# Filler products from TensorE's first instruction on, s and b as single words, and a new order of priorities in a fused attention and feed-forward kernel

## The chip, the cores and the metric

The kernel runs on one core of a Trainium2 chip. The metric is the device time of one execution in microseconds (us). TensorE (PE) multiplies, VectorE (DVE) and ScalarE (ACT) evacuate and transform, GpSimd (POOL) issues the loads that cast to 16 bits and does some copies, and SyncE (SP) issues the other DMAs.

## The reference

Attention over 8 batches and 8 heads, with a local mask in heads 0 to 3 and a strided mask in heads 4 to 7. Its output is the input of a feed-forward layer with a squared ReLU, scaled by `s` and shifted by `b`.

```python
# q, k, v: (8, 8, 576, 64); w_in: (512, 2048); w_out: (2048, 512); s, b: (1,)
scores = matmul(q, k.T) / 8
mask_local   = (rel >= 0) & (rel < 32)                 # heads 0..3, rel = row - column
mask_strided = (rel >= 0) & (row % 32 == column % 32)  # heads 4..7
attn = softmax(where(mask, scores, -1e9)) @ v
x = attn.transpose(0, 2, 1, 3).reshape(4608, 512)
h = x @ w_in
g = s * maximum(h, 0) ** 2 + b
out = g @ w_out                                        # (4608, 512) float32
```

## The kernel before

**Work.** A batch has four pairs of heads, m = 0 to 3 (0 and 1 local, 2 and 3 strided). For each pair TensorE transposes q and k (later batches, from 3 to 5 on, get this from a transposing DMA instead), makes scores against a block-diagonal copy of q (`qD_loc`, `qD_str`), ScalarE takes the exponential (`p_loc`, `p_str`), VectorE masks it (batch 0 is masked by an extra product instead), TensorE multiplies with v, which has a column of ones, and VectorE divides by that column's sums (`rec`, then `x_nat`). A transpose puts the result into `xT`.

The feed-forward layer takes the 4608 tokens in blocks T of 512. Its first product (`ff1`) has, for each of 16 slices ft of the hidden width, four products over ct (the four pairs' channels), each of 512 columns; ScalarE's ReLU gives `u`, a square gives `gT`. In the first block, ft = 0 to 3 runs with ct outermost (`FIRST`), so that its products for ct = 0 need pair 0's `xT` only. The second product (`ff2`) has 64 products of 512 columns for a block; from block 2 on (`SEVEN`) seven products of blocks take the place of eight, and so does the first product in the last two blocks. `s` is used as a per-partition scalar when the output is evacuated, `b` scales the column sums of `w_out` into `bcs`.

**Order.** The order of instructions on every engine is fixed when the kernel is built, by a planner (`Plan`, L17). It keeps a clock `t` for TensorE in ns, a time at which each other engine is free, and a table `done` of when each piece of data is there. TensorE's work comes as `Step`s with a duration, needs and a PSUM bank; evacuations come as posts with a cost for each engine that may do them. `flush` gives a post to an engine when its needs are met and the engine is free within `SLACK` of the clock; among posts that are ready, the one with the smallest ready time plus its kind's `LATER` goes first. The kind is the first entry of its key, and a key whose third entry is 0 gets nothing added. Kinds: `e` exponentials, `p` masks (in batch 0 exponentials), `u` ReLUs, `g` squares, `ev` output evacuations, `in` casts and copies of inputs, and others for the products in seven.

The main loop takes a step of attention when one is ready and attention is behind its share (`due`), else a step of `ff1`, else of `ff2`. When nothing is ready it fills TensorE with products of constants, which nothing reads (`keep_running`, L1416 on), until the next thing is expected; this is done only while fewer than 16 steps of `ff1` are out. Loads have expected landing times: a table `AT` for batch 0 (the first q at 5200), and for what follows `landing(cost)`, which adds costs to a running `ring`. The first quarter of w_in costs 2700 and gets 600 on top. The planner starts at `plan.t = 1850.0` (L1414).

**Loads at the start.** GpSimd's queue issues q, k and v of batch 0, then casts v, then issues the four quarters of w_in (`load_w_in`, L339), later batch 1 and w_out. SP's queue issues, after a small copy that waits for part of q (`gate`, L1293), the masks, then s and b, then rows of zeros for `ks` (L311):

```python
nc.sync.dma_start(out=masks, in_=h_mask.ap())
nc.sync.dma_start(out=s_sb, in_=moe_s.to_broadcast([128, 1]))
nc.sync.dma_start(out=b_sb, in_=moe_b.to_broadcast([128, 1]))
```

So s and b are each read 128 times, a word for each partition.

Lines that the prediction uses: L439 and L447 transposes of q and k, L568 scores, L629 products with v, L676 transposes of x, L928 `ff1`, L1183 `ff2`, L896 and L1153 the products in seven, L1431 fillers, L586 exponentials, L646 and L656 the division, L349 copies and casts, L1210 and L1221 the column sums of w_out.

Of the kernel before, what the change touches and what calls it, by code (L numbers as in the profile page):

```python
# [1 line left out]

# [1 line left out]

# [7 lines left out]
FP32 = mybir.dt.float32  # L12
AF = mybir.ActivationFunctionType
# [3 lines left out]
class Plan:  # L17
# [6 lines left out]

    LAT = {"A": 70.0, "V": 70.0, "P": 70.0, "D": 12000.0, "X": 7000.0, "Y": 12000.0}

    SLACK = 800.0
    LATER = {"g": 1500.0, "S": 1500.0, "in": 2500.0, "w_mix": 2500.0, "wc": 1500.0}

    def __init__(self):  # L30
        self.t = 0.0
        self.done = {}
        self.pend = []
        self.free = {"A": 0.0, "V": 0.0, "P": 7000.0, "D": 0.0, "X": 0.0, "Y": 0.0}
        self.banks = {}
# [9 lines left out]
    def flush(self):  # L45
        while True:
            best = None
            for p in self.pend:
# [3 lines left out]
                if p[1].keys() <= {"A", "V"} and min(  # L52
                        self.free[e] for e in p[1]) > self.t + self.SLACK:
                    continue
# [66 lines left out]
        self.keys, self.posts, self.after = keys, posts, after  # L121


@with_exitstack
def kernel(
    ctx: ExitStack,
# [7 lines left out]
    moe_b: bass.AP,  # L134
    out: bass.AP,
):
    nc = tc.nc
    B, H, S, D = q.shape
    NTOK, DM = out.shape
    DFF = moe_w_in.shape[1]  # L140
    stride = 32
    scale = 1.0 / float(np.sqrt(D))
    PS = 512
# [14 lines left out]
    for p in range(SQ):  # L158
        for c in range(SQ):
# [12 lines left out]
    const = ctx.enter_context(tc.tile_pool(name="consts", bufs=1))  # L172
# [11 lines left out]
    ident = const.tile([128, 128], FP16)  # L184
    masks = const.tile([128, LQ + SQ], FP16)
    mask_loc, mask_str = masks[:, 0:LQ], masks[0:SQ, LQ:LQ + SQ]
    s_sb = const.tile([128, 1], FP32)
    b_sb = const.tile([128, 1], FP32)

    w_in_sb = [const.tile([128, 4, n], FP16, name=f"w_in_sb{i}")  # L190
               for i, n in enumerate((512, 512, 512, 512))]
    w_out_sb = const.tile([128, NFT, DM], FP16)
    bcs = const.tile([128, DM], FP32)
    w_mix = {i: const.tile([128, NFT // 2, DM // 2], FP16, name=f"w_mix{i}") for i in (2, 3, 4)}
# [3 lines left out]
    part32 = w_mix[4].rearrange("p f m -> p (f m)").bitcast(FP32)[:, 64:192]  # L198
# [30 lines left out]
    x_dram = [tc.dram_tile([S, 128], FP16, name=f"x_dram{i}") for i in range(4)]  # L229

    sched = ctx.enter_context(tc.manual_schedule())
    plan = Plan()

# [102 lines left out]
    def load_w_in():  # L336
        wv = moe_w_in.rearrange("(c p) f -> p c f", p=128)
        for i, at in enumerate((0, 512, 1024, 1536)):
            nc.gpsimd.dma_start(out=w_in_sb[i], in_=wv[:, :, at:at + w_in_sb[i].shape[2]])  # L339

    def load_w_out(chunks):

# [48 lines left out]
    TB, SB, AB, F1B, F2B = 1, 2, 1, 2, 2  # L391
# [24 lines left out]
    def bank(group):  # L416
        return ps[group.name]

    def pair_steps(b, m):
# [6 lines left out]
        st = {}  # L426
# [128 lines left out]
        def score(i, group):  # L555

            g, n = i // per_s, min(per_s, nt - i // per_s * per_s)

            def f():
                if i % per_s == 0:  # L560
                    st["s", g] = bank(group)
                c = i % per_s * 2 * nq
                if b < PE_MASK:

                    nc.tensor.matmul(
                        out=st["s", g][0:nk, c:c + 2 * nq], lhsT=ident[0:nk, 0:nk],
                        rhs=neg_loc if loc else neg_str, start=True, stop=False)
                nc.tensor.matmul(  # L568
                    out=st["s", g][0:nk, c:c + 2 * nq], lhsT=(st["k"][:, i * nq:i * nq + nk] if loc else st["k"][:, i, 0:SQ]),
                    rhs=st["q"][:, i].rearrange("d e c -> d (e c)"), start=b >= PE_MASK, stop=True)  # L570

            s = Step(f, (2 if b < PE_MASK else 1) * (2 * nq / 2.4 + 8), needs=[("q", id_), ("k", id_)],
                     group=group if i % per_s == 0 else None)
            if i % per_s == n - 1:
                key = ("s", id_, g)
                s.keys = [key]

                ng = nt // per_s + (nt % per_s > 0)

                def ex(eng):  # L580
                    if g == 0:
                        st["whole"] = p_bufs[loc][p_taken[loc] % len(p_bufs[loc])]
                        p_taken[loc] += 1
                    at = g * 2 * per_s * nq
                    st["pw", g] = st["whole"][:, at:]
                    nc.scalar.activation(  # L586
                        out=st["pw", g][0:nk, 0:2 * n * nq],
                        in_=st["s", g][0:nk, 0:2 * n * nq], func=AF.Exp, scale=scale)

                def ms(eng):  # L590
                    pt = st["whole"][:, 0:2 * nt * nq].rearrange("k (t c) -> k t c", c=nq)
                    mask = (mask_loc if loc else mask_str)[:, None, :].to_broadcast(
                        [nk, 2 * nt, nq])
                    nc.vector.tensor_tensor(out=pt[0:nk], in0=pt[0:nk], in1=mask, op=ALU.mult)
# [132 lines left out]
    gts = {}  # L727
# [5 lines left out]
    H = NFT // 2  # L733
# [496 lines left out]
        return first, second, third  # L1230


    def arrive(keys, at):
        for k in keys:
            plan.done[k] = at

    ring = 0.0
# [53 lines left out]
    def after_landing(i, src):  # L1291
# [5 lines left out]
        out=v_loc[0].rearrange("p h t d -> p (h t) d")[LPAD:128, 2 * LT:4 * LT, 0:D],  # L1297
        in_=v.rearrange("b h (t p) d -> b p (h t) d", p=LQ)[0, :, 2 * LT:4 * LT])
# [9 lines left out]
    plan.done["raw", "v", False, 0] = AT["vs"]  # L1308
    after_landing(0, loaded[0, "ql"][0:1, NL // 2:NL // 2 + 1])
    nc.sync.dma_start(out=masks, in_=h_mask.ap())  # L1310
    nc.sync.dma_start(out=s_sb, in_=moe_s.to_broadcast([128, 1]))
    nc.sync.dma_start(out=b_sb, in_=moe_b.to_broadcast([128, 1]))
    def weights_in(eng):

        nonlocal ring
        nc.gpsimd.tensor_copy(out=gate[0:8, 2:3], in_=loaded[0, "qs"][64:SQ, 0:1])
        load_w_in()
        ring = 14200.0
        for keys, cost in ([0], 2700), ([1], 2500), ([2], 2500), ([3], 2500):
            arrive([("w_in", c) for c in keys], landing(cost))  # L1320

# [51 lines left out]
    f1, f2 = [], []  # L1373
    for T in range(NBLK):
        if T == 0:

            gr = [Group("s", SB, "f1", F1B) for _ in range(4)]
            cts = FIRST
            f1 += [ff1(T, ft, ct, gr[ft], cts, True) for ct in cts for ft in range(4)]
        for ft in ff_order(T)[0 if T else 4:] if T < FIRST7 else ():  # L1380
            gr = Group("f1", F1B, "f2", F2B) if T == 0 else Group("f1", F1B)
            for ct in range(4):
                f1.append(ff1(T, ft, ct, gr))
        if T == FIRST7:
            f1 += ff1_seven()
        if T == 0:

            gr = [Group(*x) for x in [("f2", F2B), ("f2", F2B), ("s", SB), ("f2", F2B)]]
            sums = bcs_steps(Group("s", SB))
            for c in range(0, NFT, 4):  # L1390
                if c >= NFT - 8:
                    f2.append(sums[c // 4 - 2])
                f2 += [ff2(T, ts, ft, gr[ts]) for ts in range(2) for ft in range(c, c + 4)]
            f2.append(sums[2])
            f2 += [ff2(T, ts, ft, gr[ts]) for ts in (2, 3) for ft in range(NFT)]
            for i, s in enumerate(f2):
                s.pos = 1.25 * (i + 1) / len(f2)
            mix_post()
            continue
        if T >= SEVEN:  # L1400
            f2 += ff2_seven(T)
            continue
        for ts in range(4):

            parts = 2 if T == NBLK - 1 and ts == 3 else 1
            for part in range(parts):
                gr = Group("f2", F2B)
                for ft in range(NFT):
                    f2.append(ff2(T, ts, ft, gr, part, parts))
                    f2[-1].pos = T + 0.25 + (ts + (part + ft / NFT) / parts) / 4  # L1410
    combine_w()
    for T in range(FIRST7, NBLK):
        combine_x(T)
    plan.t = 1850.0  # L1414

    def keep_running(until):  # L1416

# [20 lines left out]
    f1_pos = [i / 64.0 if i < cut else FIRST7 + (i - cut) / 112.0 for i in range(len(f1) + 1)]  # L1438
# [3 lines left out]
    i1 = i2 = first = 0  # L1442

    def due():

        pos = f1_pos[i1] + (f2[i2 - 1].pos if i2 else 0.0) + 0.1
        return (pos if pos <= 1 else 1 + (pos - 1) / 2) * batch_ns

    while i2 < len(f2) or any(at_i[p] < len(att[p]) for p in range(len(att))):
# [6 lines left out]
        for p in active:  # L1456
            r = plan.step_ready(att[p][at_i[p]])
# [4 lines left out]
        order = []  # L1462
# [14 lines left out]
        if cand is not None and (att_done < due() or main is None):  # L1477
            s = att[cand][at_i[cand]]
# [11 lines left out]
    while plan.pend:  # L1490
        plan.flush()
        if plan.pend:
            plan.advance()


# [28 lines left out]
```

## Time and profile before

| | |
|---|---|
| median of 6 runs | 300.73 us (300.67 to 301.1) |
| the profiled execution's own time | 300.7 us |
| its span, first to last instruction | 298.9 us |
| mean granted clock of TensorE | 0.992 |
| TensorE busy | 290.7 us, 97% |
| VectorE, ScalarE, GpSimd busy | 237.0, 191.9, 94.5 us |
| DMA moved | 38.19 MB, mean 128 GB/s |

Times inside the execution count from the span's start. A line of waits gives who waited, for whom, the sum in us, how often, and the longest. A line of a timeline gives start, length, engine, line, operation, output and inputs, shape, count, and in brackets the idle time ahead and what ended it; consecutive products overlap in it, so the rate of products is read from their starts. The granted clock is the share of TensorE's full rate. The time outside the span is the difference of 300.7 and 298.9.

### The profile page before, as it was taken

The numbers are of one execution on the slowest core, as the hardware profiler recorded it, in microseconds if no ns is written. First come the engines' busy times: TensorE is split into PE (matmuls) and PEld (weight loads), VectorE is DVE, ScalarE is ACT, GpSimd is POOL, SyncE is SP. The second block draws the span as 40 slices with busy tenths as digits, with TensorE's granted clock in tenths as the row PEclk, the third lists the DMA queues.
The fourth block names the chain that finished last, engine by engine and source line by source line (L and its number), as shares of the span: only waits on it lengthen the run. The fifth ranks groups of instructions, "written<-read, shape, count | busy, mean of one in ns | idle before, by whom it ended". The sixth has DMA issues, their size and how long they took to land.

```text
span 298.9 us, 7101 instructions
## 1 busy us (share of the span) xinstructions
PE 290.7 (97%) x2800; PEld 219.8 (74%) x2800; DVE 237.0 (79%) x500; ACT 191.9 (64%) x335; POOL 94.5 (32%) x141
## 2 busy tenths in 40 slices
PE   6989999999999999999999999999999999999995
PEld 3764665666556567889867786778888989999984
DVE  5854797888886789767986798779898788888963
ACT  3574884898727797646783887378977545675400
POOL 8873343610860197008820593110001000000000
PEclk9998999999999999999999999999999999999999
DMA  7999999999999599999999999996120200210214
GB/s 133 153 206 203 170 218 194 172 197 131 126 169 171 88 113 127 146 193 107 162 152 192 134 148 160 128 167 171 43 77 20 95 30 20 70 37 1 92 53 141
DMA packets 106436, 38.19 MB, mean 128 GB/s; under 512 B 85698, under 2 KB 104258, under 8 KB 106402
## 3 DMA queue, kind: packets, MB, share of 16 engines
q0 software_dynamic: 60848, 18.23, 63.1%
q1 hardware_dynamic: 45554, 19.51, 34.8%
q8 instruction: 22, 0.36, 0.5%
q14 instruction: 12, 0.10, 0.1%
HBM read 36.99 MB, written 10.62 MB: 159 GB/s over the span
## 4 chain that ended last, share of the span: by engine, by line
PE 91%; DMA 3%; POOL 3%; ACT 1%; issue 1%; DVE 0%; POOLq 0%; ACTq 0%; DVEq 0%
PE ps_f L928 32%; PE ps_f L896 25%; PE ps_f L1183 8%; PE ps_s L568 5%; DMA w_in_sb<-in_moe_w_in_dram 3%; PE ps_f L1153 3%; PE ps_a L629 2%; PE ps_t L1153 2%; PE ps_a L1153 2%; PE ps_s L896 2%; PE ps_s L1153 2%; PE ps_t L629 1%; PE ps_t L896 1%; PE ps_s L1183 1%; PE ps_t L447 1%; PE ps_s L928 1%
## 5 line engine op out<-in xcount | busy, mean ns | idle before, releaser
L928 PE MATMUL ps_f<-xT,w_in_sb 128*128 128x512 f16 (+4 forms) x568 | 116.3, 333 | 0.0
L954 ACT ACTIVATE u<-ps_f 128x512 f16<-128x512 f32 x107 | 62.8, 594 | 34.2 <-PE ps_f L928 33.7
L928 PEld LDWEIGHTS <-w_in_sb 128*128 128x128 f16 x576 | 57.7, 114 | 24.3 <-issue 2.3
L896 PEld LDWEIGHTS <-gT 128*128 128x128 f16 x608 | 58.4, 98 | 9.6
L896 PE MATMUL ps_f<-w_out_sb,gT 128*128 128x256 f16 x376 | 54.9, 273 | 0.0
L1183 PE MATMUL ps_f<-w_out_sb,gT 128*128 128x512 f16 x112 | 29.4, 379 | 0.0
L586 ACT ACTIVATE p_str<-ps_s 72x432 f16<-72x432 f32 (+1 forms) x45 | 20.4, 483 | 8.8 <-PE ps_s L568 8.3
L962 ACT ACTIVATE gT<-u 128x1024 f16<-128x1024 f16 x24 | 25.4, 1058 | 0.7
L964 DVE TENSOR_TENSOR gT<-u 128x1024 f16<-128x1024 f16 x32 | 22.1, 690 | 4.4 <-ACT u L954 3.9
L896 PE MATMUL ps_f<-w_mix,gT 128*128 128x256 f16 x176 | 24.9, 273 | 0.0
L656 DVE TENSOR_TENSOR x_nat<-ps_a,rec 96x384 f16<-96x384 f32 (+2 forms) x46 | 23.9, 519 | 0.6
L586 ACT ACTIVATE p_loc<-ps_s 128x384 f16<-128x384 f32 x46 | 21.4, 495 | 4.6 <-PE ps_s L568 4.1
L764 DVE TENSOR_TENSOR gT<-gT 128x1024 f16<-128x1024 f16 x34 | 22.6, 680 | 0.7 <-ACT gT L962 0.6
L327 POOL DMA_DIRECT2D v_loc<-in_v_dram x24 | 17.9, 766 | 6.8 <-DMA w_out_sb<-in_moe_w_out_dram 3.8
L896 PEld LDWEIGHTS <-S 128*128 128x128 f16 x176 | 17.1, 98 | 3.0
L1183 PEld LDWEIGHTS <-gT 128*128 128x128 f16 x128 | 11.6, 98 | 9.5 <-issue 0.7
L646 DVE RECIPROCAL rec<-ps_a 96x6 f32<-96x6 f32 (+2 forms) x46 | 8.4, 182 | 11.4 <-PE ps_a L629 11.2
L629 PEld LDWEIGHTS <-p_str 72*128 72x128 f16 x256 | 13.3, 98 | 5.5
L1254 POOL COPY gate<-kT 1x1 f16<-1x1 f16 x6 | 2.3, 390 | 45.4 <-DMA kT<-ks 45.4
L332 POOL DMA_DIRECT2D v_str<-in_v_dram x16 | 13.0, 816 | 10.7 <-PE ps_a L629 3.7
L896 PE MATMUL ps_f<-w_mix,S 128*128 128x256 f16 x112 | 15.7, 273 | 0.0
L1094 ACT ACTIVATE gT<-u 128x1024 f16<-128x1024 f16 x13 | 13.8, 1058 | 1.7 <-DVE u L1073 1.4
(234 smaller groups left out, 529.7 us busy)
## 6 DMA issues: line engine op xcount, KB each, us to landing
out_dram<-o SPq DMA_DIRECT2D x34, 256.0 KB, 2.3
w_in_sb<-in_moe_w_in_dram POOLq DMA_DIRECT2D x4, 512.0 KB, 11.3
w_out_sb<-in_moe_w_out_dram POOLq DMA_DIRECT2D x4, 512.0 KB, 11.6
qs<-in_q_dram POOLq DMA_DIRECT2D x6, 288.0 KB, 7.3
ks<-in_k_dram POOLq DMA_DIRECT2D x6, 288.0 KB, 8.9
v_loc<-in_v_dram POOLq DMA_DIRECT2D x24, 72.0 KB, 9.7
ql<-in_q_dram POOLq DMA_DIRECT2D x4, 288.0 KB, 10.5
kl<-in_k_dram POOLq DMA_DIRECT2D x16, 72.0 KB, 3.5
```

Source lines behind the costliest of these rows:

```text
L327: nc.gpsimd.dma_start(out=vl[LPAD:128, h, :, 0:D], in_=v_band(b, h))
L586: nc.scalar.activation(out=st["pw", g][0:nk, 0:2 * n * nq], in_=st["s", g][0:nk, 0:2 * n * nq], func=AF.Exp, scale=scale)
L629: nc.tensor.matmul(out=st["pa", g][:, n % 6, :], lhsT=st["pw", gp_][0:nk, i * nq:i * nq + WIDE], rhs=vt[0:nk, 2 * mm + e, j, :])
L656: nc.vector.tensor_tensor(out=x_at(0, cnt), in0=st["pa", g][0:nq, 0:cnt, 0:D], in1=st["rec", g][0:nq, 0:cnt].to_broadcast([nq, cnt, D]), o ...
L764: {"V": nc.vector, "P": nc.gpsimd}[eng].tensor_tensor(out=at(out), in0=at(x), in1=at(y), op=op)
L896: nc.tensor.matmul(out=gts[name, T, t][:, 0] if halves else gts[name, T][:, t], lhsT=lhs(k, t), rhs=rhs(k), start=fresh and k == 0 and (ha ...
L928: nc.tensor.matmul(out=gts["h", T, ft][:, lo:hi], lhsT=w_in_sb[ft // 4][:, ct].rearrange("p (x l) -> p l x", l=4)[:, ft % 4], rhs=xT[ct][: ...
L954: nc.scalar.activation(out=u, in_=gts["h", T, ft], func=AF.Relu)
L962: nc.scalar.activation(out=g, in_=u, func=AF.Square)
L964: nc.vector.tensor_tensor(out=g, in0=u, in1=u, op=ALU.mult)
L1153: nc.tensor.matmul(out=st[bk][:, 256 * t:256 * t + 256], lhsT=lhs(t, c), rhs=rhs(c), start=fresh and t == c == 0, stop=t == c == 1, skip_g ...
L1183: nc.tensor.matmul(out=gts[id_], lhsT=gts[T][:, ft, ts * 128:(ts + 1) * 128], rhs=w_out_sb[:, ft, cols], start=(ft == 0), stop=(ft == NFT ...
```

## The change

It does these things:

- The planner starts at 1050 instead of 1850, with its table of landing times as it was, so products of constants are planned for a longer stretch before the first q is due. The base of the running landing time for w_in goes from 14200 to 13200.
- s and b come as one word each into one partition (`sb_row`). A new first step of `ff2`, `sb_step`, multiplies a row of 1/32 with the two words, which gives 128 partitions of s/32 and b/32 in PSUM; ScalarE copies them with a scale of 32 into `sb_all`, whose columns are now `s_sb` and `b_sb`. Its data is expected at 16000.
- The priorities come from a table of 25 kinds, where there were five; `SLACK` goes from 800 to 600. The share that attention is kept ahead (0.1) stays. A search over such tables is in the code but set to zero tries; the kernel is laid out once with stand-ins for its objects and once in earnest, both when it is built.
- The buffer for a pair's exponentials is taken by whichever group of them is placed first.

```diff
-    SLACK = 800.0
-    LATER = {"g": 1500.0, "S": 1500.0, "in": 2500.0, "w_mix": 2500.0, "wc": 1500.0}
-
-    def __init__(self):
+    def __init__(self, order):
         self.t = 0.0
+        self.SLACK, self.ahead, self.LATER = order["SLACK"], order["ahead"], order
...
+ORDER = {"g": 0.0, "S": 1500.0, "in": 2500.0, "w_mix": 2500.0, "wc": 2500.0, "ev": -400.0,
+         "e": 1500.0, "fu": -400.0, "Ub": 1000.0, "c22": 500.0, "c11": -800.0, "fv": -1500.0,
+         "u": -400.0, "c12": 2500.0, "fe": -800.0, "Va": 1000.0, "xc": 0.0, "Ua": -1500.0,
+         "k": 500.0, "x": 0.0, "Vb": 0.0, "p": 1000.0, "C22": 500.0, "q": 0.0, "c21": -800.0,
+         "SLACK": 600.0, "ahead": 0.1}
...
+ORDERS = 0
...
-    s_sb = const.tile([128, 1], FP32)
-    b_sb = const.tile([128, 1], FP32)
+    sb_row = const.tile([1, 2], FP32)
+    sb_all = const.tile([128, 2], FP32)
+    s_sb, b_sb = sb_all[:, 0:1], sb_all[:, 1:2]
...
-                    if g == 0:
+                    if "whole" not in st:
                         st["whole"] = p_bufs[loc][p_taken[loc] % len(p_bufs[loc])]
...
+    def sb_step():
+
+        group = Group("s", SB, "f2", F2B)
+
+        def f():
+            gts["sb"] = bank(group)[:, 0:2]
+            nc.tensor.matmul(out=gts["sb"], lhsT=part32[0:1, :], rhs=sb_row, start=True, stop=True)
+
+        def g(eng):
+            nc.scalar.activation(out=sb_all, in_=gts["sb"], func=AF.Copy, scale=32.0)
+
+        return Step(f, 150, needs=[("sb_row",)], group=group, keys=[("sb_ps",)],
+                    posts=[([("sb_ps",)], {"A": 250.0}, g, [("sb",), group])])
+
...
-    nc.sync.dma_start(out=s_sb, in_=moe_s.to_broadcast([128, 1]))
-    nc.sync.dma_start(out=b_sb, in_=moe_b.to_broadcast([128, 1]))
+    nc.sync.dma_start(out=sb_row[0:1, 0:1], in_=moe_s[None, :])
+    nc.sync.dma_start(out=sb_row[0:1, 1:2], in_=moe_b[None, :])
+    plan.done["sb_row",] = 16000.0
...
-        ring = 14200.0
+        ring = 13200.0
...
+            f2.append(sb_step())
...
-    plan.t = 1850.0
+    plan.t = 1050.0
...
-        pos = f1_pos[i1] + (f2[i2 - 1].pos if i2 else 0.0) + 0.1
+        pos = f1_pos[i1] + (f2[i2 - 1].pos if i2 else 0.0) + plan.ahead
```

More of the change, by code (lines that the diff above doesn't have):

```diff
@@ L1 @@
 from contextlib import ExitStack
+import random
 import numpy as np
@@ L121, in __init__, with varied, __getattr__, __call__ @@
         self.keys, self.posts, self.after = keys, posts, after
+ORDER = {"g": 0.0, "S": 1500.0, "in": 2500.0, "w_mix": 2500.0, "wc": 2500.0, "ev": -400.0,
[3 rows of a table added]
+         "SLACK": 600.0, "ahead": 0.1}
+KINDS = ("g", "S", "in", "w_mix", "wc", "Va", "Ua", "Ub", "Vb", "C22", "xc", "q", "k", "r", "x", "e",
+         "p", "u", "ev", "fv", "fu", "fe", "c11", "c22", "c21", "c12")
+def varied(order, rnd):
+    order = dict(order)
+    for kind in rnd.sample(KINDS, rnd.choice((1, 2, 4))):
+        order[kind] = rnd.choice((-1500.0, -800.0, -400.0, 0.0, 500.0, 1000.0, 1500.0, 2500.0))
+    if rnd.random() < 0.2:
+        order["SLACK"] = rnd.choice((400.0, 600.0, 800.0, 1000.0))
+    if rnd.random() < 0.2:
+        order["ahead"] = rnd.choice((0.0, 0.05, 0.1, 0.2))
+    return order
+class Nothing:
+    def __getattr__(self, name):
+        if name.startswith("__"):
+            raise AttributeError(name)
+        return self
+    def __call__(self, *args, **kw):
+        return self
+    def __getitem__(self, at):
+        return self
+ORDERS = 0
 @with_exitstack
@@ L136, with lay_out @@
 ):
[L137 to L140, printed above, removed]
+    shapes = q.shape, out.shape, moe_w_in.shape
+    nothing = [Nothing()] * 11
+    rnd = random.Random(0)
+    best = ORDER
+    end = lay_out(*nothing, best, *shapes)
+    for _ in range(ORDERS):
+        other = varied(best, rnd)
+        at = lay_out(*nothing, other, *shapes)
+        if at < end:
+            best, end = other, at
+    lay_out(ctx, tc, tc.nc, q, k, v, moe_w_in, moe_w_out, moe_s, moe_b, out, best, *shapes)
+def lay_out(ctx, tc, nc, q, k, v, moe_w_in, moe_w_out, moe_s, moe_b, out, order, q_shape, out_shape,
+            w_in_shape):
+    B, H, S, D = q_shape
+    NTOK, DM = out_shape
+    DFF = w_in_shape[1]
     stride = 32
@@ L231 @@
     sched = ctx.enter_context(tc.manual_schedule())
-    plan = Plan()
+    plan = Plan(order)
     NL, NS = 4 * LT * D, 4 * ST * D
@@ L338, in load_w_in @@
         for i, at in enumerate((0, 512, 1024, 1536)):
-            nc.gpsimd.dma_start(out=w_in_sb[i], in_=wv[:, :, at:at + w_in_sb[i].shape[2]])
+            nc.gpsimd.dma_start(out=w_in_sb[i], in_=wv[:, :, at:at + 512])
     def load_w_out(chunks):
@@ L1493 @@
             plan.advance()
+    return plan.t
 _INS = ['q', 'k', 'v', 'moe_w_in', 'moe_w_out', 'moe_s', 'moe_b']
```

## The prediction

> **What bounds the kernel now.** I read the page first, for who is busy, then TensorE's waits in two stretches, because a share over the whole span hides where its few gaps lie.
>
> ```profile
> span 298.9 us, 7101 instructions
> PE 290.7 (97%) x2800; PEld 219.8 (74%) x2800; DVE 237.0 (79%) x500; ACT 191.9 (64%) x335; POOL 94.5 (32%) x141
> PEclk9998999999999999999999999999999999999999
> ```
>
> TensorE is busy 97% of the span, and the one slice of its clock below 9 is the fourth, 22.4 to 29.9 us. The waits, first up to 25 us, then from 25 us on:
>
> ```profile
> PE ps_t L439 <- DMA ql<-in_q_dram: 1.3, 1, 1.3
> PE ps_s L1431 <- DVE w_mix L261: 1.1, 1, 1.1
> PE ps_s L928 <- DMA w_in_sb<-in_moe_w_in_dram: 0.9, 1, 0.9
> PE ps_a L676 <- DVE x_nat L656: 0.5, 1, 0.5
> PE ps_f L568 <- DVE kTs L349: 0.4, 1, 0.4
> ```
>
> ```profile
> PE ps_t L1153 <- ACT E L349: 0.3, 1, 0.3
> ```
>
> Five waits before 25 us, one of 0.3 us in the 274 us behind. From 25 us on the end is set by the sum of TensorE's products; nothing can be won there except the 0.3 us (some 1.0 us when I add all gaps between starts of products beyond their own length). So any gain must come from the head, and it counts only if more real work is done by 25 us. The chain of waits names the head's longest piece, the first quarter of w_in:
>
> ```profile
> 10.49 8.54 DMA w_in_sb<-in_moe_w_in_dram
> ```
>
> Why 8.5 us for 1 MB read? Windows of 1 us (columns: stretch, length, busy time of PE, PEld, DVE, ACT and POOL, TensorE's granted clock, share of the DMA engines, GB/s):
>
> ```profile
> 12.00:13.00 1.00, 1.00 (x22) 1.00 (x20) 0.95 (x3) 1.00 (x7) 1.00 (x3) 1.00 1.31 175
> 13.00:14.00 1.00, 1.00 (x28) 0.92 (x24) 0.99 (x3) 1.00 (x4) 0.96 (x2) 1.00 0.51 65
> 14.00:15.00 1.00, 0.58 (x9) 0.42 (x8) 0.91 (x3) 0.74 (x2) 0.45 (x2) 1.00 0.31 62
> 15.00:16.00 1.00, 1.00 (x25) 1.00 (x23) 0.56 (x3) 0.57 (x2) 1.00 (x3) 1.00 1.18 202
> ```
>
> There is a hole from 13 to 15 us: 65 and 62 GB/s, 202 after it. In the trace's packets the software queue (w_in is next on it) moves its last v row at 13.71, then nothing until 14.30, and is at full rate at 15.0. In just that time SP's queue moves 4-byte packets, 312 from 12.7 to 15.3 us: the 256 single words of s_sb and b_sb (128 partitions each) and 56 semaphore writes. On one engine after the other the last such packet is followed within 10 ns by the first row of w_in.
>
> What the late weights do to TensorE is seen in windows laid on the clock's steps:
>
> ```profile
> 17.96:21.38 3.42, 2.02 (x35) 1.25 (x32) 2.32 (x9) 2.39 (x11) 2.19 (x4) 1.00 1.24 206
> 21.38:24.79 3.41, 3.41 (x14) 1.41 (x14) 0.02 (x1) 1.22 (x3) 0.56 (x1) 0.50 1.24 207
> ```
>
> TensorE is short of work in the first window (it waits for w_in from 17.96 to 19.07 and for x_nat from 20.38 to 20.99) and then runs at half clock for 3.41 us, with real products:
>
> ```profile
> 19.07 0.41 PE L928 MATMUL ps_s<-xT,w_in_sb 128*128 128x512 f16 x1 [0.94 <-DMA w_in_sb<-in_moe_w_in_dram]
> 22.15 1.06 PE L928 MATMUL ps_s<-xT,w_in_sb 128*128 128x512 f16 x2
> 25.62 4.48 PE L928 MATMUL ps_f<-xT,w_in_sb 128*128 128x512 f16 x20
> ```
>
> Those start 427 ns apart at 22 us, 216 ns at 25.6 us. Lost by starts: 1.1 (w_in) + 0.6 (x_nat) + 1.7 (3.41 at half clock) + 0.1 of fillers (two of 128 columns at 20.25) = 3.5 us. That is what this change can reach.
>
> **The words of s and b.** Removed: 256 packets; added: two. The hole's upper price is (204-65)+(204-62) = 281 KB, at 204 GB/s 1.4 us (204 is the mean of 202 to 207 behind it; masks and zeros, which stay, are already in the 65 and 62). Its lower price: the packets' own time, 256 x 9 ns / 16 engines = 0.14 us. I take 1.2, near the upper end, because the software queue is empty in exactly that time and each engine restarts when its words are through. So w_in's first quarter lands at 19.03 - 1.2 = 17.8 us, and all that is queued behind it (batch 1, w_out) as much earlier. A rule speaks against this: the Trainium skill, "DMA: Bandwidth & Descriptors", section "Queues, rings and completion order", says that an engine takes turns between its queues packet by packet; by that the words would cost w_in about the 0.14 us, and the 1.2 would be nearly nothing.
>
> SP issues two DMAs as before (0.57 and 0.60 us), so the zeros behind them go out when they did; w_in's own issue at 10.49 stays, because GpSimd's queue has no gap from 1.30 to 10.36. Added on TensorE: one float32 product of 2 columns. Bounds: products of 65 columns start 0.03 us apart, the float32 product of 512 columns lasts 0.59 us; I take 0.1, near the small one. It waits for the words; planned at 16000, some 16.5 us, while b_sb landed at 15.6 behind all its packets, so the wait is nothing; were it late, attention's scores would stand behind it. ScalarE's copy of 2 columns: an x_nat copy of 64 columns takes 0.23 us, off the path (s and b are first read at 54 us).
>
> **Fillers.** The planner's clock starts at 1050 instead of 1850, so before the first load's due time (5200) it fits 9 of 512 columns and a shorter one where there were 7 and two shorter: about 0.75 us more at the half clock. Today the fillers end at about 4.5 us and real work starts at 5.86, when ql has landed (5.81). They fill part of that 1.3 us: 0 us. Without that cover they would cost 0.75. Since the plan stands at 5.2 to 5.3 in either kernel when ql lands, all behind it keeps its offset: plan 17500 was 17.97 us in the trace, plus 0.47.
>
> **The due time of w_in.** The base goes from 14200 to 13200, so the first hidden product may be queued from 16500, about 17.0 us, wherever no step of attention is ready. Behind it stand the last scores and the value products of the fourth pair, whose results the rest of T=0's first group needs. With w_in at 17.8 the wait is between 0 (placed late) and 0.8 us; I take 0.5, the middle, instead of 1.1: -0.6. The chain behind (ScalarE's p_str ends at 18.7, so value products could follow then, today they run from 19.3 to 20.1) still leaves the 0.6 us for x_nat; I give it -0.2, from fillers that turn into products and value products that go sooner.
>
> **The clock.** With eight products of 0.216 us (those that need only the first two pairs) instead of the three that started there, the window before 21.38 has about 1.1 us more work. The window from 4.31 to 7.72 had a wait of 1.3 in 3.41 and kept the clock; this one would have about 1.1. So I count the whole half-clock loss as gone: -1.7. Here too a rule speaks otherwise: the Trainium skill, "TensorE: Matmul & The Clock Gate", section "Why this matters for your kernels", asks only that no idle gap exceed about 3 us. No gap here did (1.1 and 0.6), and the clock fell all the same; the trace decides, but by the rule the clock would not hang on the gaps, that term would be zero and the sum -0.6.
>
> **Priorities and slack.** They reorder ScalarE's, VectorE's and GpSimd's work and its releases on TensorE. Gain: at most the 1.0 us of gaps after 25 us. Loss: gaps of 0.25 to 0.45 us are what the trace shows when an evacuation comes late; one of 0.3 in each of the eight batches would be 2.4 us. I take 0, since both engines have room (79% and 64%), and keep -1.0 and +2.4.
>
> **What is late next.** The first output product starts at 40.75, w_out's first quarter landed at 39.98: 0.77 us of room. With loads 1.2 and TensorE 2.4 us earlier the room is -0.4; batch 1's attention can fill it (its transposes started 1.6 to 3.2 us after their data landed), so 0 to 0.4, I take 0.1. Later there is room: at 53.8 us some 31 products of T=0's output are left, 6.7 us.
>
> **Sum.** -0.6 -0.2 -1.7 +0.1 +0.1 = -2.3. The profiled execution took 300.7 with a span of 298.9, so 1.8 lies outside: 296.6 + 1.8 = 298.4 us. It equals the median (300.73) within 0.1. Ends of this case: 297.2 (no wait for w_in, chain 0.6 shorter, s and b's product hidden) to 299.4 (hole worth 0.8, wait 0.8, 0.4 lost at w_out).
>
> **Rivals.** (1) The gain is handed back: the words go, but the window before 21.4 stays thin and the clock falls anyway, or attention of batch 0 is the bound. For: x_nat's wait has nothing to do with w_in. Against: eight products are there to fill. Then -0.8 + 0.2 = -0.6: 300.1, at best 299.6. (2) Slower: the words are not what stops w_in. It lands at 18.9, while its product is queued from 17.0; TensorE waits 1.9 instead of 1.1 with scores and value products behind it, and the clock falls: 300.7 + 0.8 = 301.5. This decides from a landing of 18.1 on, where the longer wait eats the earlier landing. For: the rule on queues; against: the empty software queue. (3) The new order makes stalls in the steady part: at eight times 0.3 us it ends at 298.4 + 2.4 = 300.8 or, with the clock lost too, at 302.5. For: 25 priorities are set at once. Against: room on both engines, and 0.3 us of waits under the present order.
>
> **Numbers.** Forecast 0.62, rival (1) 0.16, (2) 0.12, (3) 0.10. What a measurement of this kernel can tell from no change is about 0.2%, 0.6 us. Faster by more: 0.62 + 0.10 of (1) = 0.72; within: 0.06 of (1), 0.03 of (2), 0.02 of (3) = 0.11; slower: 0.09 + 0.08 = 0.17. The range runs from 297.0, just under the forecast's best end, to 300.8, which takes in (1) and the near end of (3); (2) and the rest of (3) are left out.
>
> **What would show it.** Right: no hole at 13 to 15 us, w_in's first quarter landing by 18.0, a granted clock of 1.0 from 4.3 us to the last product, products of 512 columns 216 ns apart at 22 us, and few waits after 25 us. Wrong: a landing at 18.9 (the words were innocent), the clock at 0.5 somewhere before 30 us (the 1.7 is not won), a wait on w_out at 38 to 40 us over 0.4, or a sum of TensorE's waits after 25 us well above 1 us.

## The result

The changed kernel takes 299.22 us (median of 38 runs, 298.62 to 301.0) against 300.64 us for the kernel before (77 runs); the ratio is 0.9963, interval 0.9955 to 0.9971, that is 1.1 us faster. The means (299.42 and 300.53 us) give the same 1.1, the medians 1.4. The forecast was 298.4, 2.3 us faster than the profiled execution of before. The direction came as forecast and so did the lead at 25 us; the gain at the end was about half.

The whole page of after first, the three lines that answer to those of before:

```profile
span 298.6 us, 7089 instructions
PE 290.7 (97%) x2802; PEld 219.6 (74%) x2802; DVE 236.9 (79%) x504; ACT 191.7 (64%) x334; POOL 91.8 (31%) x139
PEclk9999999999999999999999999999999999999999
```

The clock no longer falls. In the clock's step where before's TensorE was short of work (busy 2.02 of 3.42 us), after's is busy 3.28 of 3.41:

```profile
19.22:22.63 3.41, 3.28 (x36) 1.92 (x35) 1.16 (x4) 2.50 (x9) 1.73 (x4) 1.00 1.24 207
```

Yet the span is only 0.3 us shorter than before's 298.9. This execution took 300.42 us, 1.2 more than its kernel's median, so one profile will not do. First the hole in the loads, by windows of 1 us (last two columns: share of the DMA engines, GB/s):

```profile
12.00:13.00 1.00, 1.00 (x24) 1.00 (x22) 0.95 (x3) 1.00 (x6) 1.00 (x2) 1.00 1.29 194
13.00:14.00 1.00, 0.95 (x25) 0.78 (x21) 0.95 (x4) 1.00 (x4) 0.96 (x2) 1.00 1.19 192
14.00:15.00 1.00, 0.53 (x11) 0.53 (x12) 0.78 (x2) 0.64 (x2) 0.17 (x1) 1.00 1.21 194
15.00:16.00 1.00, 1.00 (x25) 1.00 (x22) 0.72 (x3) 0.73 (x2) 0.95 (x2) 1.00 1.21 200
```

192 and 194 GB/s stand where before had 65 and 62. Of the four quarters of w_in the first is on its way for the shortest time, 8.5 us in before and 7.0 in after (first line before, second after):

```profile
DMA to landing us min/median/max: 8.5/11.3/14.1
DMA to landing us min/median/max: 7.0/10.2/13.3
```

So it lands at 17.43 us instead of 19.02. TensorE's waits in after, up to 25 us and then from 25 us on:

```profile
PE ps_s L1502 <- DVE w_mix L316: 1.1, 1, 1.1
PE ps_f L623 <- DVE kTs L404: 0.5, 1, 0.5
PE ps_f L684 <- ACT p_str L641: 0.3, 1, 0.3
...
PE ps_t L494 <- DMA ql<-in_q_dram: 0.8, 1, 0.8
PE ps_a L684 <- DVE p_loc L649: 0.3, 1, 0.3
PE ps_f L951 <- DVE o L882: 0.3, 1, 0.3
PE ps_t L1208 <- ACT E L404: 0.2, 1, 0.2
```

The waits for w_in and x_nat are gone from the head. New behind 25 us are a wait of 0.8 us for q of batch 1 and two of 0.3 us, which lie at 201 to 203 us. The timeline of after's TensorE shows the first of them:

```profile
22.18 0.59 PE L983 MATMUL ps_f<-xT,w_in_sb 128*128 128x512 f16 x2
22.61 0.60 PE L983 MATMUL ps_s<-xT,w_in_sb 128*128 128x512 f16 x2
23.04 3.83 PE L983 MATMUL ps_f<-xT,w_in_sb 128*128 128x512 f16 x17
27.70 0.45 PE L494 MATMUL ps_t<-ident,ql 96*64 96x96 f16 x12 [0.82 <-DMA ql<-in_q_dram]
```

Two products take 0.43 us at 22 us (22.18 to 22.61), 215 ns each, where before had 427. Then TensorE is too early for batch 1.

To say how far ahead one execution is of another, I lay their products in order, count 1 column as 1/2.4 ns (512 columns start 215 ns apart above), leave the fillers out, and compare the times at which the same sum of work has been started. By that measure after is 2.58 us ahead of before's profile at 25 us of before's time, 1.75 behind the wait for q, 1.2 to 1.4 from 45 to 180 us, 0.3 at 206 us and 0.64 at its last product. So the head gave 2.6, where 2.4 was forecast, and places behind it took most of that: q of batch 1, the stretch up to the first product with w_out, and 201 to 206 us.

### The profile page after: what moved, and what is told of

Read it like the earlier page. It is cut to its first block, busy times and chain, and to the rows that moved or that the text cites. A ratio compares the mean times of both kernels' runs of the same rounds, so it can differ in the third digit from the quotient of the medians.

```text
span 298.6 us, 7089 instructions
## 1 busy us (share of the span) xinstructions
PE 290.7 (97%) x2802; PEld 219.6 (74%) x2802; DVE 236.9 (79%) x504; ACT 191.7 (64%) x334; POOL 91.8 (31%) x139
## 4 chain that ended last, share of the span: by engine, by line
PE 77%; DMA 15%; POOL 4%; DVE 2%; issue 1%; ACT 0%; POOLq 0%; DVEq 0%
PE ps_f L983 25%; PE ps_f L951 22%; PE ps_f L1238 8%; DMA v_loc<-in_v_dram 5%; DMA qs<-in_q_dram 4%; PE ps_s L623 4%; DMA w_out_sb<-in_moe_w_out_dram 4%; PE ps_f L1208 3%; PE ps_a L684 2%; DMA vs<-in_v_dram 2%; PE ps_t L1208 2%; PE ps_s L951 2%; PE ps_a L1208 2%; PE ps_s L1208 2%; PE ps_t L951 1%; PE ps_s L1238 1%
## 5 line engine op out<-in xcount | busy, mean ns | idle before, releaser
L1009 ACT ACTIVATE u<-ps_f 128x512 f16<-128x512 f32 x103 | 60.4, 594 | 34.4 <-PE ps_f L983 33.8
L1017 ACT ACTIVATE gT<-u 128x1024 f16<-128x1024 f16 x30 | 31.7, 1058 | 0.8
L641 ACT ACTIVATE p_loc<-ps_s 128x384 f16<-128x384 f32 x46 | 20.8, 493 | 4.9 <-PE ps_s L623 4.7
L1019 DVE TENSOR_TENSOR gT<-u 128x1024 f16<-128x1024 f16 x26 | 17.6, 678 | 1.6 <-ACT u L1009 1.3
L1323 POOL COPY gate<-kT 1x1 f16<-1x1 f16 x6 | 1.6, 259 | 45.8 <-DMA kT<-ks 45.8
L1149 ACT ACTIVATE gT<-u 128x1024 f16<-128x1024 f16 x12 | 12.7, 1058 | 2.1 <-DVE u L1128 1.4
```

Of the source, the lines that this page charges most:

```text
L641: nc.scalar.activation(out=st["pw", g][0:nk, 0:2 * n * nq], in_=st["s", g][0:nk, 0:2 * n * nq], func=AF.Exp, scale=scale)
L1009: nc.scalar.activation(out=u, in_=gts["h", T, ft], func=AF.Relu)
L1017: nc.scalar.activation(out=g, in_=u, func=AF.Square)
L1019: nc.vector.tensor_tensor(out=g, in0=u, in1=u, op=ALU.mult)
```

## The experiments

Times are medians; each ratio is to the kernel before on the same chip. "Ahead" is the measure above, against before's first profile. A wait given "by starts" counts from where the next product would have started, and is some 0.2 us longer than the idle time in a line of waits.

| run | us | ratio, interval |
|---|---|---|
| after_again | 299.57 | 0.9971, 0.9951 to 0.9991 |
| long_fill | 299.64 | 0.9983, 0.9964 to 1.0002 |
| old_prio | 300.06 | 0.9986, 0.9964 to 1.0009 |
| before_wout_ahead | 299.74 | 0.9987, 0.9961 to 1.0012 |
| ql_later | 300.41 | 0.9996, 0.9977 to 1.0016 |
| prio_words | 300.28 | 1.0006, 0.9983 to 1.0028 |
| words_back | 301.07 | 1.0010, 0.9987 to 1.0033 |
| fill_only | 300.54 | 1.0015, 1.0001 to 1.0029 |
| sb_only | 301.81 | 1.0043, 1.0016 to 1.0069 |
| wout_ahead | 302.91 | 1.0064, 1.0040 to 1.0089 |
| words_twice | 301.93 | 1.0066, 1.0043 to 1.0090 |
| prio_only | 302.06 | 1.0067, 1.0052 to 1.0083 |
| sb_wout | 302.24 | 1.0084, 1.0066 to 1.0102 |
| wout_ql | 303.91 | 1.0096, 1.0067 to 1.0125 |
| start_due | 303.91 | 1.0124, 1.0105 to 1.0142 |

### The same two kernels again

No edit. Two more profiles of before:

> The kernel before once more, one look. TensorE's clock is set in steps of 3.41 us whose phase differs from run to run (full rate came at 4.3, 5.4, 5.6, 9.2 and 10.5 us in the executions so far). Theory (the phase decides): the step to full rate is elsewhere than 4.31 us, and if it is at 5 to 8 us the first real work at 5.4 runs at half rate for a while; the fall at 21.4 us may be missing. Rival (the fall belongs to this kernel's order): full rate by 4.5 and the fall at 21 to 25 us again.

> The same, for one more phase. Theory: another pair of steps than in the look before it, and the time within 299.5 to 302.0 us as the phase has it. Rival: the same steps.

before_look (300.92 us, span 299.1) had the fall again, from 21.68 to 25.09 us. before_look2 (300.23, span 298.5) had none: its granted clock is 1.0 from 9.32 us on, and at 25 us it is 1.29 us ahead of the first profile. Its waits from 25 us on, and the place in its timeline:

```profile
PE ps_f L1183 <- DMA w_out_sb<-in_moe_w_out_dram: 0.8, 1, 0.8
PE ps_t L1153 <- ACT E L349: 0.3, 1, 0.3
```

```profile
40.45 0.61 PE L1183 MATMUL ps_f<-w_out_sb,gT 128*128 128x512 f16 x2 [0.81 <-DMA w_out_sb<-in_moe_w_out_dram]
```

Without the fall TensorE is too early for w_out and waits until its first quarter lands (40.40); 0.47 of the 1.29 us are left. The fall covered this wait. The runs' mean clocks say the same over many executions: of 117 runs of before beside the experiments, 25 have a mean granted clock of 0.988 to 0.994 and a median of 300.97 us, the other 92 (0.998 to 1.0) 300.24. The fall is worth 0.74 us where it happens, and it happens in one execution of five. (The 77 runs of the result have no clocks on record.) None of 52 runs of the changed kernel is below 0.997.

Two more profiles of the changed kernel:

> The changed kernel once more, for its typical profile. Theory (the head gains some 2.6 us by 25 us, and 0.8 to 1.0 of it is given back where batch 1's q is planned before it lands): 299.2 us, with TensorE ahead of the kernel before by 2.4 to 2.7 us at 25 us and by about 1.2 from 35 us to the end, the wait of 0.8 us on ql at 27 us there again, and no gap of 0.5 us at 201 to 203 us. Rival (what was lost at 201 to 203 us belongs to the new order): that gap is there again, and TensorE ends 0.6 ahead.

> The changed kernel, a third profiled execution. By the theory that the head wins some 2.6 us by 25 us in every clock phase and that the landing of w_out's first quarter (38.8 to 39.5 us in the two executions seen) takes part of it back, TensorE is ahead of the first profile of before by 2.2 to 2.8 us at 25 us, the first product of the second layer starts within 0.1 us of that landing, and the span lies between 296.5 and 298.6 us, the two seen. If the loss of about 1 us near 200 us of the first of them is a chance of the execution and not of the order, it may be there or not; if it belongs to the order, it is there again.

Both took the time of the forecast: spans of 296.5 and 296.6 us (298.45 and 298.4 us for the execution). At 25 us they are 2.59 and 2.58 ahead, from 45 to 180 us 2.0 to 2.4, at the last product 2.7 and 2.56. The waits of after_look from 25 us on:

```profile
PE ps_f L1238 <- DVE rec L701: 0.3, 1, 0.3
PE ps_t L1208 <- ACT E L404: 0.2, 1, 0.2
```

The 0.3 us on `rec` stand in front of the first product with w_out, which starts at 38.94, just behind the landing. Neither of the two executions waits for q of batch 1, and neither loses at 200 us. So the loss there belongs to the execution, not to the order of instructions. Where it starts is seen on GpSimd's queue, first after, then after_look (`gate` is a copy of one element of kT that GpSimd must do before it may issue the last batch's loads):

```profile
171.52 0.62 POOL L1323 COPY gate<-kT 1x1 f16<-1x1 f16 x1 [18.25 <-DMA kT<-ks]
172.30 0.18 POOL L1323 COPY gate<-kT 1x1 f16<-1x1 f16 x1 [0.16 <-DMA kT<-ks]
...
180.06 2.99 POOL L382 DMA_DIRECT2D v_loc<-in_v_dram  x4
```

```profile
167.84 0.18 POOL L1323 COPY gate<-kT 1x1 f16<-1x1 f16 x1 [15.91 <-DMA kT<-ks]
168.50 0.18 POOL L1323 COPY gate<-kT 1x1 f16<-1x1 f16 x1 [0.48 <-DMA kT<-ks]
...
176.27 2.98 POOL L382 DMA_DIRECT2D v_loc<-in_v_dram  x4
```

The transposing DMA of k lands 3.8 us later in after, though after's TensorE is behind by only 0.9 us there, and v is issued 3.8 us later. VectorE then stands in front of v's cast, in after and in after_look:

```profile
196.23 0.32 DVE L404 COPY v_loc<-v_loc 32x640 f16<-32x640 f16 x1 [2.65 <-DMA v_loc<-in_v_dram]
```

```profile
193.80 0.33 DVE L404 COPY v_loc<-v_loc 32x640 f16<-32x640 f16 x1 [1.09 <-DMA v_loc<-in_v_dram]
```

VectorE's order is fixed and it has no gap behind the cast, so all that follows is late with it, and 5.5 and 6.8 us on TensorE waits:

```profile
201.75 0.93 PE L951 MATMUL ps_f<-w_out_sb,gT 128*128 128x256 f16 x7 [0.31 <-DVE o L882]
203.02 0.36 PE L684 MATMUL ps_a<-v_loc,p_loc 128*128 128x65 f16 x6 [0.35 <-DVE p_loc L649]
```

Each pair of transposing DMAs holds SP's queue for a while. The four pairs between 149 and 170 us hold it for 3.84 to 5.51 us each in after and 2.56 to 4.26 in after_look, 17.5 and 13.9 us in all; the last pair, first after, then after_look:

```profile
165.86 3.84 SPq L565 DMA_TRANSPOSE kT<-ks  x2
162.92 2.56 SPq L565 DMA_TRANSPOSE kT<-ks  x2
```

Why they are slower in one execution than in another of the same program, no run settles.

### The words

```diff
-    nc.sync.dma_start(out=s_sb, in_=moe_s.to_broadcast([128, 1]))   # and b_sb
+    nc.sync.dma_start(out=sb_row[0:1, 0:1], in_=moe_s[None, :])     # and sb_step
```

sb_only does this alone in before; words_back undoes it alone in the changed kernel:

> The kernel before with nothing but s and b as single words. Theory (the words held up w_in): no hole at 13 to 15 us, w_in's first quarter at 17.4 to 17.8 us, the clock kept; since w_in and batch 1's q are then due after they land (w_in 17.97, q some 27.9 us), nothing is given back: 298.3 to 299.0 us, as fast as the whole change or faster. Rival (the words cost their own 0.14 us): w_in at 18.9, the clock falls, 300.5.

> The changed kernel with s and b spread by the DMA again, 128 words each. Theory: the hole is back, w_in lands at 19.0 with its product queued from about 17, TensorE waits 1.0 to 2.0 us, the clock falls after it: 300.5 to 301.5 us. Rival (the gain is that of the order and the due times): 299.2.

words_twice is before with b spread over 128 partitions twice more, 256 packets that nothing reads, the order as it was:

> The kernel before with b spread by the DMA two times more, into a scratch tile that nothing reads: 512 single words instead of 256, order and everything else as before. Theory (single words stop w_in's queue, some 1.3 us for 256, and w_out's landing sets the second layer's start): the hole from 13 to 15 us grows to 16, w_in's first quarter lands at 20.0 to 20.6 and w_out's at 40.9 to 41.7, 301.3 to 302.0 us. Rival (their own 0.14 us): 300.5, no change.

In words_back the hole is back, and TensorE waits for q of batch 1 behind it:

```profile
13.00:14.00 1.00, 1.00 (x30) 0.95 (x26) 0.99 (x3) 1.00 (x4) 0.96 (x2) 1.00 0.60 75
14.00:15.00 1.00, 0.47 (x8) 0.36 (x7) 0.92 (x3) 0.81 (x2) 0.70 (x2) 1.00 0.52 87
```

```profile
PE ps_t L493 <- DMA ql<-in_q_dram: 1.2, 1, 1.2
```

In words_twice it is about twice as long:

```profile
13.00:14.00 1.00, 1.00 (x13) 0.92 (x12) 0.99 (x5) 0.84 (x5) 0.96 (x2) 1.00 0.48 55
14.00:15.00 1.00, 1.00 (x32) 1.00 (x30) 0.97 (x3) 1.00 (x5) 0.45 (x2) 1.00 0.13 10
15.00:16.00 1.00, 0.61 (x10) 0.36 (x6) 0.95 (x4) 1.00 (x3) 1.00 (x3) 1.00 0.75 111
16.00:17.00 1.00, 0.97 (x21) 0.97 (x22) 0.54 (x2) 0.56 (x2) 1.00 (x2) 1.00 0.95 139
17.00:18.00 1.00, 1.00 (x16) 0.92 (x15) 0.96 (x3) 0.75 (x3) 1.00 (x3) 1.00 1.01 162
```

Against 204 GB/s these five windows lack 149 + 194 + 93 + 65 + 42 = 543 KB, 2.7 us; before lacked 281 KB, 1.4 us, by the same working. So 256 packets of 4 bytes cost some 1.3 us, once and twice. The second quarter of w_in lands 1.5 us later than in before (23.07 for 21.55), w_out's first 2.8 later (42.81), and the kernel is 2.0 us slower. The words are guilty, and their price is near the upper bound of 1.4 us that the prediction gave; it took 1.2. Late weights also bring the clock's fall: five of the six runs of words_twice have a mean granted clock of 0.988 to 0.994, against 3 of 23 runs of before on that chip.

Yet sb_only is slower than before, and three of its 12 runs still show a mean clock of 0.991 to 0.994. Its w_in lands at 17.51 and it is 1.47 us ahead from 25 to 52 us; it loses 0.8 at 54 to 57 us, around the transposes of batch 2's k, and 1.0 at 203 us:

```profile
PE ps_s L569 <- DMA kT<-ks: 0.9, 1, 0.9
```

words_back keeps the whole rest of the change and is 1.0010 where the change is 0.9963: the words are worth 0.4 to 0.5% within the change, and nothing, or less, without it. But words_back's head is 2.73 us ahead at 25 us with w_in at 18.73, as far as the changed kernel's: the head's gain did not need the early landing. What the early landing buys comes later, at q of batch 1 (words_back waits 1.3 us by starts) and at w_out (landing at 40.24, a wait of 0.7 us by starts).

### The order, part by part

```diff
# fill_only, in before                  # start_due, in before
-    plan.t = 1850.0                    -    plan.t = 1850.0
+    plan.t = 1050.0                    +    plan.t = 1050.0
                                        -        ring = 14200.0
                                        +        ring = 13200.0
# prio_only, in before: the 25 priorities and SLACK 600
# prio_words: prio_only and sb_only together
# old_prio, in the changed kernel: the five old priorities and SLACK 800
# long_fill, in the changed kernel: plan.t = 450.0
```

> The kernel before with the planner's start at 1050 alone: two more filler products of 512 columns, all else as before. Theory (fillers decide how often the clock rises before real work begins): 0.4 to 1.0 us faster in the median, 299.6 to 300.2, and full rate by 5.6 us in the look. Rival (the forecast's value): 300.6, no change, since they end before ql lands.

> The kernel before with the new start of the fillers and the new due time alone; words and priorities as before. Theory (the head's gain is given back at w_out's landing, 40.2 us on the mean with 256 words): 300.2 to 300.9 us. Rival (the due time saves the 1.1 us wait for w_in and keeps it): 299.6.

> The kernel before with the 25 new priorities and the slack of 600 alone; words, fillers and due times as before. Theory (priorities are worth 0 within 0.4): 300.4 to 300.8 us. Rival (they account for the 0.5 us between the changed kernel and the one with old priorities): 299.8 to 300.2 us, with fewer waits behind 200 us.

> The kernel before with the single words and the new priorities and slack, but with the old start of the fillers and the old due time of w_in. Theory (the new order fits loads that come 1 us earlier; start and due time are worth 0.3 to 0.5): 299.4 to 300.1 us. Rival (the due time is what fits): 301.5 or more, as either of its two parts alone.

> The changed kernel with the five old priorities and the old slack of 800. Theory (priorities moved nothing that counts): 299.2 us within 0.4, w_in at 17.4, clock 1.0, the wait on ql at 27 us still there. Rival (the new priorities shorten the head's chain from scores to xT): over 300 us, with the first 12 first-layer products of 512 columns done later than 23 us.

> The changed kernel with the planner's start at 450 instead of 1050, so that fillers reach the landing of q (5.1 to 5.9 us). Theory (with no gap there the clock rises by 5.8 in every phase, but the time is set later by w_out): 299.0 to 299.7 us, with fewer runs over 300. Rival (the longer fillers hold up the first transposes when q lands at 5.1): 299.9 or more.

None of the parts wins alone. fill_only's profile has no clock fall and is 1.63 us ahead at 25 us, and waits 1.0 us for w_out, much as before_look2 does (0.8). Yet 4 of its 12 runs have a mean clock of 0.992 to 0.994, so fillers alone do not take the fall away. start_due is 2.14 ahead at 25 us and loses all of it and more: by starts 1.5 us for q of batch 1, 1.2 at 48 to 57 us, and 2 at 196 to 201 us behind a ReLU. prio_only stands longest at w_out (which lands at 40.76):

```profile
PE ps_f L1183 <- DMA w_out_sb<-in_moe_w_out_dram: 1.5, 1, 1.5
```

and loses 1.0 more from 52 to 62 us, where k of batch 2 lands at 55.09. The same priorities with single words (prio_words) are 0.4% better than single words alone, with intervals that overlap, and still wait 0.6 for w_out. With the change's early loads but the old priorities (old_prio) the ratio is 0.9986; the new ones have 0.9971 and 0.9963. The profiled old_prio also got its full clock only at 10.47 us, which took 1.8 us, so what the priorities are worth there stays open. A still longer stretch of fillers (long_fill) gives its full clock at 3.77 us and no more time.

### Who is late next

```diff
# wout_ahead (changed kernel), before_wout_ahead (before), sb_wout (sb_only)
+        weights_out([0])            # ahead of batch 1's strided v
...
-        weights_out(range(4))
+        weights_out([1, 2, 3])
# ql_later (changed kernel): loads behind w_in are expected 1000 ns later
+        ring += 1000.0
# wout_ql: wout_ahead and ql_later together
```

> The changed kernel with w_out's first quarter issued ahead of batch 1's strided v instead of behind it (288 KB that pass it). Theory (the landing of w_out's first quarter sets when the second layer starts, and eats what the head has won): it lands at 37.7 to 38.6 us instead of 38.8 to 39.5, the wait in front of the first second-layer product goes under 0.1, and TensorE keeps 0.2 to 0.5 us more: 298.8 to 299.2. Rival (attention's v is as urgent): the strided v lands 2.4 us later and a wait on it takes the place: 299.6 or more.

> The kernel before with the same swap and nothing else. Theory (in executions whose clock does not fall, the kernel before waits 0.8 to 1.1 us for w_out's first quarter, and gives its luck back there): 0.3 to 0.8 us faster than before in the median, and no wait in front of the first second-layer product. Rival (the fall of the clock at 21 to 25 us is what costs): no change.

> Before with the two words sent as single words and spread by TensorE, and the first quarter of w_out issued ahead of batch 1's strided v; priorities, due times and the planner's start as before. With single words alone the ratio was 1.0043, with w_out's quarter ahead alone 0.9987 (unclear). If what takes the earlier w_in back in the old order is the landing of w_out, both together give a ratio below 0.997 and no wait for w_out; if it is the old order itself (evacuations near 54 us and batch 2's loads), the head is about 1.5 us ahead at 40 us, it is lost by 60 us, and the ratio is 1.000 to 1.005.

> The changed kernel with all loads behind w_in due 1000 ns later in the plan, as they were before the change. Theory (batch 1's q is planned at 26.87 us and lands at 26.2 to 27.9): no wait on ql at 27 us in any execution, worth 0 to 0.8, in the median 0.2 to 0.4: 299.0 to 299.4. Rival (w_out's landing eats it all the same): 299.6, no change.

> Both of these on the changed kernel. Theory: their gains add, 298.5 to 299.0 us. Rival (either one is given back at the loads of batch 2 at 54 to 58 us or of the last batch at 200 us): 299.4.

The waits for w_out and for q could each be taken away or made smaller, and none of that became time. In wout_ahead the quarter lands at 38.65 and TensorE doesn't wait for it. But the changed order loses 1.3 us at 147 us, behind VectorE (`x_nat` and `Va`), 3.1 at 196 to 205 us, 2.5 of it to transposing DMAs, and 0.8 more at 236 us behind VectorE's `qD_loc`:

```profile
PE ps_s L623 <- DMA kT_alt<-kl: 1.4, 2, 1.2
PE ps_s L623 <- DMA kT<-ks: 1.1, 1, 1.1
PE ps_s L1208 <- DVE qD_loc L1083: 0.8, 1, 0.8
```

In ql_later the wait for q shrinks to 0.26 us by starts and the one for w_out grows to 0.99. wout_ql still waits 1.0 us for w_out and loses 2.25 us at 198 us in front of a ReLU; its last batch's gate passes at 176.2 us, the latest of all. before_wout_ahead is the best of the variants of before, and its gain is within the interval. sb_wout, profiled in its fastest run, is 2.2 to 2.3 ahead up to 120 us and loses 1.5 at 145 to 147 us around the strided scores, with waits for VectorE; that is neither of the two cases expected for it, and its median is 2 us above that run. In the profiles of these variants the head is ahead at 25 us by 1.07 to 2.6 us, and the time is lost later: at w_out, behind VectorE near 147 us, and at 196 to 205 us, where transposing DMAs or a ReLU come late. I did not find what in a new order makes these late.

## Why the prediction was half right

**The words: right.** 1.2 us was predicted for the hole; the landing moved by 1.6, and doubling the packets confirmed 1.3 us for 256. The 0.14 us set against it was an estimate from 9 ns for a word's packet and from the rule of turns packet by packet in the Trainium skill ("DMA: Bandwidth & Descriptors", "Queues, rings and completion order"); these runs show ten times as much. Whether the turns or the 9 ns are at fault they do not tell.

**w_in's due time, fillers, sum of the head: right in sum, in part by luck.** Forecast 2.4 us ahead by 25 us, measured 2.58, 2.59 and 2.58. But words_back has 2.73 without the early landing, so the terms behind the sum are not shown one by one. Fillers alone, forecast at 0, are 0.4 us slower (fill_only 1.0015, the interval just above 1). Which part keeps the clock up is open: with words alone (3 of 12 runs) or fillers alone (4 of 12) it falls about as often as in before, and the profiles of fill_only and before_look2 without a fall are executions of kernels that have it; in words_back it fell in 1 of 12, in old_prio in none of 12.

**The clock, -1.7: mis-sized, the first step that failed at the end of the span.** It was real between 21.38 and 24.79 us of that execution. But it was read from one execution of a kind that is one in five, and it was priced at its place, not at the end. Behind it the same execution had 0.77 us of room at w_out, because of the loss; where the clock holds, before_look2 and fill_only wait 0.8 and 1.0 us there. At the end the fall is worth 0.74 us, and over all executions 25/117 x 0.74 = 0.16 us. With 0.74 for the 1.7, the sum would be -1.3 and the forecast 299.4, near the 299.22 measured; that is agreement in size, not proof, for two executions did reach 298.4. The prediction took the agreement of the profile with the median of six runs (0.1 us) for a sign that the profile was typical; over 117 more runs the median is 300.36. The 77 of the result, without clocks on record, have 300.64.

**What is late next, +0.1: mis-sized, the second.** In all three profiles of the changed kernel the first product with w_out starts within 0.05 us of the landing (39.53, 38.83 and 38.89 us), so a load, not TensorE, sets that place: there, from 40 to 42 us, the lead falls by 0.4 in the two that did not wait for q (after_again and after_look) and by 0.2 in the one that did. By 45 us it has fallen from 2.6 to 2.1 or 2.2, and to 1.2 where q of batch 1 came late as well. That second wait is a side of an edit that the prediction did not follow: the base of `ring` moves the due times of everything behind w_in by 1000 ns too, and q's transposes were placed for a landing at some 26.9 us by the trace's time, while q landed at 27.66, 26.23 and 26.34 in the three. Of the signs of being wrong that were named, one showed: the waits after 25 us sum to 1.6 us in after, against 0.4 and 0.5 in the other two.

**Priorities, 0 with +2.4 as the far end.** On before's loads they cost 2.0 us, near that end, so rival (3) has the size of the part, though not of the whole, and not its reason: the largest loss in prio_only is one wait of 1.5 us for w_out, not 0.3 us in each batch. Parts that were summed one by one do not add: single words +0.4%, priorities +0.7%, start and due time +1.2%, all together -0.4%. That fits an order made for one set of landing times, with which half of the change disagrees; no run shows that this is the reason.

**Rivals.** (2), the words innocent, fell by the landing and by words_twice. (1), the gain handed back, had 0.6 us, nearer to the 1.1 measured than the forecast's 2.3, but not its reason: it was not the clock that took the rest, but q of batch 1, w_out and the last batch's v, as far as the profiles show. The profiled execution that took 300.42 lost 0.8 us to q and about 1 us to v; the two at 298.4 lost neither. The median lies 0.8 above these two, about one such loss; the executions between were timed and not profiled, so which loss they have is open.

## What to carry to other kernels

Profile the kernel before more than once before a loss in it is counted as a gain: the runs' mean clocks tell cheaply how often it is there. Price a loss at the next load behind it, since a late engine makes its own room: subtract the wait that appears when it comes early. In this case parts of the change that moved the order or the landing times alone lost time; move them together, and follow every due time that hangs on a shared base.

## What the runs showed of the hardware

Two loads of one word to 128 partitions on one queue cost another queue's load 1.3 us: for 2 us the DMA moved 65 and 62 GB/s in place of 204, and 55 and 10 with 512 packets.

The granted clock changes on steps of 3.41 us, and their phase differs from execution to execution: full rate came at 4.31, 4.61 and 9.32 us in three profiles of before, and at 3.77 to 10.47 in all. It fell behind a window of 3.42 us with idle gaps of 1.1 and 0.6 us in it; the Trainium skill ("TensorE: Matmul & The Clock Gate", "Why this matters for your kernels") warns only of gaps over about 3 us. The two falls profiled came behind windows in which TensorE was busy 2.02 us (before) and 2.04 (before_look) of 3.42. It stayed up behind 2.10 of 3.41 (before, from 4.31 us) and behind 2.03 of 3.42 (wout_ql, from 5.29 us), so these runs give no threshold. With full rate at 9 or 10 us a profile is 1.0 to 1.8 us later at 11 us than before's first, which had it at 4.31.

The same program's transposing DMAs held SP's queue for 3.84 us a pair in one execution and 2.56 in another (kT<-ks). Four such pairs took 3.6 us longer in all, and the last batch's loads, which wait for them, came 3.8 us later.
